# Attention and two expert layers on one core: first expert's weights behind the last pair's copies, routing of batch 0 from unit 64 on, two expert blocks with half of their second layer in plain fp32

## The chip, the core and the metric

The program runs on one core of a Trainium2 chip. Its engines work side by side, each through its own list of instructions: TensorE for matrix products (PE; PEld is its weight load), VectorE (DVE), ScalarE (ACT), GpSimd (POOL) and SyncE (SP), which here issues most of the DMA transfers. The metric is the time of one execution on the device in microseconds (us), the median over runs.

## What is computed

Attention feeds a layer of routed experts, which feeds a layer in which every token uses every expert. All of it is fp32.

```python
# q, k, v: 2 batches, 8 heads, 576 rows, 64 columns
q_rot, k_rot = rotate(q), rotate(k)
scores = scale * q_rot @ k_rot.T
attn = softmax(scores)
x = (attn @ v)            # -> 1152 tokens x 512

# experts 1: D=512, F=1024, E=8, one expert a token
logits = normed(x) @ normed(expert_emb).T / tau
expert_idx = argmax(logits, axis=1)
for e in range(E):
    mask = expert_idx == e
    h = maximum(x[mask] @ w1[e], 0)
    out[mask] = gate_w[mask] * (h @ w2[e])

# experts 2: all experts, weights P by 8 rounds of row and column scaling
for e in range(E):
    out += P[:, e:e+1] * (maximum(x @ w1[e], 0) @ w2[e])
```

## The kernel before

**Attention** works on eight pairs of heads. A head has five tiles of rows (four of 120, one of 96), so that a pair makes ten units, and units k = 0 to 79 run in one loop. A unit computes scores (L245), their maxima on DVE (L251), the exponentials on ACT (L257), transposes them (L279) and multiplies with the values (L302). The operands of pair i, kd and qd, are laid out ahead, during pair i - 1: POOL splits the numbers (L217) and SP copies them, kd in the unit with k % 10 = 3 (L226) and qd in that with k % 10 = 5 (L224). Pair 7 starts with unit 70.

**Routing** of batch 0 runs beside the loop. `route_half(0)` is a generator of small DVE instructions, some products and a few DMAs; once a unit, `next(trickle)` (L719) runs it to its next yield, behind the exponentials of the unit before and ahead of this unit's scores. It finds each token's expert (L470 to L474), ranks the tokens of each expert with products of triangles of ones (rp, L479 to L481), picks the expert with most tokens (`choose`, L419), reads its number into a register of SP and issues eight loads of that expert's weights, four of w1 and four of w2, 512 KB each (`fetch`, L83, into raw1 and raw2). `pre_tokens` then gathers 128 of its tokens on POOL (L458), and `pre_x` (L647) transposes them into xp. `take_out` takes these tokens out of the counts.

**The pre-block** computes those 128 tokens ahead of the routing of batch 1, in plain fp32, directly from the weights as they are loaded: `pre_l1` in eight pieces (L660), `pre_turn` (ReLU and transposes, L668 to L673), `pre_l2` in eight pieces (L680).

**The blocks.** After batch 1 is routed, `blocks` (L546 to L554) works out which expert each of nine blocks of 128 tokens belongs to, and `run_blocks` (L993) works through them. Here fp32 products are made of three cheaper ones: a matrix is split into a rounded part and the rest (weights: whi by an ACT copy at L843, wlo by a DVE subtraction at L836, two pieces for w1 and two for w2 in a block; tokens xh, xl at L861 and L862; hidden h into hh and hl at L888 and L889), and the products are hi with hi, lo with hi and hi with lo (L871 for layer 1, L901 for layer 2). In step i of the loop PE does the first layer of block i, the transposes of block i + 1's tokens (L858) and the second layer of block i - 1, while DVE, ACT and SP prepare the weights of the block after. `expert(i, ...)` loads the weights of block i only if its expert is another than that of block i - 1; whether it is, a register decides, and SP passes through the instruction in either case. A ninth block of four groups of at most 32 tokens, with loads of its own (qw, L923), is worked into the gaps. The pieces raw_77 and raw_78 hold w1, raw_79 and raw_80 w2.

**Order.** On PE, DVE, ACT and POOL instructions run in the order of the code, on SP too up to the head of the blocks. A load on SP waits until its target is free, and all that stands behind it on SP waits as well. Each DMA of SP also waits for the one eight before it.

**The end.** From about 353 us on the second expert layer runs (L1414, L1468), with PE busy without a gap.

## Time and profile before

| | us |
|---|---|
| median of 3 runs (1127.18 to 1128.1) | 1127.88 |
| profiled execution, its own time | 1128.22 |
| its span, first to last instruction | 1126.4 |
| PE busy, of the span | 1092.8 (97%) |
| DVE busy | 777.3 (69%) |
| ACT busy | 454.2 (40%) |
| POOL busy | 146.9 (13%) |
| mean granted clock of PE | 0.990 |

The shares are means over stages that differ. A stretch in which PE is not busy is where time may be lost, and the timeline tells what ended it: in brackets behind an instruction stands the idle time of its engine ahead of it and what released it. A releaser is inferred, and a wait for several things is put down to the one that came last by the profile. The granted clock is 1.00 at 2.4 GHz and 0.50 at 1.2 GHz.

### The profile page before, as it was taken

How to read it: one execution, taken by the hardware profiler on the slowest of the kernel's cores; microseconds unless marked ns; L12 is line 12 of the kernel's file. 1: busy time of each engine (PE TensorE's matmuls, PEld its weight loads, DVE VectorE, ACT ScalarE, POOL GpSimd, SP SyncE). 2: the span in 40 equal slices, each digit the busy share in tenths (PEclk: the TensorE clock that was granted, in tenths of full speed). 3: DMA queues.
4: the chain of work that ended last, by engine and by line, in shares of the span. 5: the costliest groups of instructions: out<-in, count | busy, mean ns of one | idle time of the engine just before them, and what ended most of it. 6: DMA issues, size and time to landing. Idle time of an engine off the chain costs nothing.

```text
span 1126.4 us, 16853 instructions
## 1 busy us (share of the span) xinstructions
PE 1092.8 (97%) x6588; PEld 926.4 (82%) x6589; DVE 777.3 (69%) x1277; ACT 454.2 (40%) x739; POOL 146.9 (13%) x115
## 2 busy tenths in 40 slices
PE   8999869999998999999999999999999999999998
PEld 4777655676766998999889998899988999899986
DVE  5767855988644488766776667766777667776665
ACT  4666625668653452233222332233322333223320
POOL 7664400253201000400000000000000000000000
PEclk9999989999998999999999999999999999999999
DMA  8676541165786011111111111111111111111102
GB/s 243 175 185 190 150 157 43 61 258 216 287 291 177 23 56 38 38 56 39 56 38 38 58 46 48 38 39 56 51 45 38 42 53 57 38 38 49 28 1 84
DMA packets 74980, 102.05 MB, mean 91 GB/s; under 512 B 5128, under 2 KB 46600, under 8 KB 74128
## 3 DMA queue, kind: packets, MB, share of 16 engines
q1 hardware_dynamic: 72528, 94.09, 27.4%
q0 software_dynamic: 1760, 5.77, 1.5%
q8 instruction: 54, 0.88, 0.3%
q10 hardware_dynamic: 608, 1.07, 0.3%
q14 instruction: 30, 0.25, 0.1%
HBM read 106.08 MB, written 7.60 MB: 101 GB/s over the span
## 4 chain that ended last, share of the span: by engine, by line
PE 67%; DMA 1%; DVE 0%; SPq 0%; ACT 0%; issue 0%
PE o L1468 35%; PE d L1414 30%; PE d L1431 2%; DMA g<-yd 1%; PE o L1358 0%; PE d L1311 0%; DVE acc L1479 0%; PE o L1389 0%; SPq L1297 0%; DVE st L1445 0%; DVE h L1456 0%; ACT h L1455 0%; PE o L1311 0%; PE o L1377 0%; PE o L1364 0%
## 5 line engine op out<-in xcount | busy, mean ns | idle before, releaser
L1468 PE MATMUL o<-w,h 128*128 128x512 f32 x1728 | 399.6, 390 | 0.3 <-DVE acc L1479 0.3
L1468 PEld LDWEIGHTS o<-w,h 128*128 128x128 f32 x1728 | 322.1, 188 | 66.2 <-DVE acc L1479 0.7
L1414 PE MATMUL d<-yq,w 128*128 128x288 f32 x2520 | 340.0, 294 | 0.0
L1414 PEld LDWEIGHTS d<-yq,w 128*128 128x128 f32 x2520 | 336.8, 188 | 2.6 <-ACT st L1442 0.2
L1479 DVE SCALAR_TENSOR_TENSOR acc<-o,P,acc 128x512 f32<-128x512 f32 x252 | 189.1, 751 | 77.1 <-PE o L1468 76.5
L1180 ACT ACTIVATE w<-raw 128x512 fp32r<-128x512 f32 x124 | 70.8, 574 | 129.9 <-DVE raw L1225 129.9
L1456 DVE SCALAR_TENSOR_TENSOR h<-st,h 128x576 fp32r<-128x576 f32 x90 | 68.0, 755 | 52.7 <-ACT h L1455 52.6
L1455 ACT ACTIVATE h<-st 128x576 fp32r<-128x576 f32 x90 | 61.5, 683 | 98.0 <-DVE st L1445 98.0
L836 DVE TENSOR_TENSOR wlo<-raw,whi 128x2048 fp32r<-128x2048 f32 x36 | 81.9, 2289 | 24.3 <-ACT whi L843 23.1
L1442 ACT ACTIVATE st<-d 128x576 f32<-128x576 f32 x90 | 58.7, 652 | 91.0 <-PE d L1414 89.0
L251 DVE TENSOR_REDUCE nb<-s 120x1 f32<-120x576 f32 (+1 forms) x80 | 60.3, 754 | 46.7 <-PE s L245 34.1
L1455 ACT ACTIVATE h<-d 128x576 fp32r<-128x576 f32 x38 | 24.7, 650 | 160.1 <-PE d L1414 158.0
L1445 DVE TENSOR_TENSOR st<-st,d 128x576 f32<-128x576 f32 x90 | 67.4, 749 | 23.9 <-PE d L1414 23.7
L257 ACT ACTIVATE p<-s,nb 120x576 f32<-120x576 f32 (+1 forms) x80 | 59.1, 739 | 60.3 <-DVE nb L251 57.7
L1181 DVE TENSOR_TENSOR w<-raw,w 128x512 fp32r<-128x512 f32 x124 | 76.9, 622 | 0.4 <-ACT w L1180 0.4
L245 PE MATMUL s<-kd,qd 128*120 128x288 f32 x280 | 55.5, 322 | 12.9 <-DMA wgk<-wg 9.6
L843 ACT ACTIVATE whi<-raw 128x2048 fp32r<-128x2048 f32 x32 | 61.3, 1917 | 14.4 <-PE h L871 9.9
L1456 DVE SCALAR_TENSOR_TENSOR h<-d,h 128x576 fp32r<-128x576 f32 x38 | 28.8, 757 | 53.7 <-ACT h L1455 53.7
L245 PEld LDWEIGHTS s<-kd,qd 128*120 128x120 f32 x280 | 39.4, 182 | 25.5 <-issue 14.5
L302 PE MATMUL o<-ph,vr 120*64 120x288 f32 x320 | 46.9, 418 | 0.0
L1241 DVE TENSOR_TENSOR w<-raw,w 128x1024 fp32r<-128x1024 f32 x32 | 39.2, 1225 | 5.6 <-ACT w L1240 5.6
L285 DVE COPY ph<-pt 120x480 f32<-120x480 f32 x64 | 41.4, 647 | 1.9 <-PE pt L279 1.9
(322 smaller groups left out, 1074.0 us busy)
## 6 DMA issues: line engine op xcount, KB each, us to landing
raw<-w1a SPq DMA_DIRECT2D x36, 512.0 KB
raw<-w2a SPq DMA_DIRECT2D x36, 512.0 KB
raw<-w1b SPq DMA_DIRECT2D x64, 256.0 KB
raw<-w2b SPq DMA_DIRECT2D x32, 512.0 KB
qw<-w1a SPq DMA_DIRECT2D x16, 512.0 KB
qw<-w2a SPq DMA_DIRECT2D x16, 512.0 KB
kd<-hl SPq DMA_DIRECT2D x28, 288.0 KB
r<-qk SPq DMA_DIRECT2D x6, 1152.0 KB
```

The source lines that it names most:

```text
L245: T.matmul(s[:m, h, :HS], qd[:, j, t * QT:t * QT + m], kd[:, j, x, h * HS:(h + 1) * HS], start=(x == 0), stop=(x == 1))
L251: V.tensor_reduce(nb[:m], s[:m, :, :HS], axis=AX.XY, op=ALU.max, negate=True)
L836: V.tensor_tensor(lo, raw, hi, op=ALU.subtract)
L843: A.activation(hi, raw, AF.Copy)
L1180: A.activation(hi, src, Copy)
L1181: V.tensor_tensor(lo, src, hi, op=ALU.subtract)
L1414: T.matmul(d[1][:, q, :QW], wv[:, wx, which, k], yq[yx][:, YQ[p], k, q * QW:(q + 1) * QW], start=new and k == 0 and (wx, yx) == (0, 0), st ...
L1445: V.tensor_tensor(halves(st[x]), halves(st[x]), mid(d), op=ALU.add)
L1455: A.activation(hi, src, AF.Relu)
L1456: V.scalar_tensor_tensor(lo, src, 0.0, hi, op0=ALU.max, op1=ALU.subtract)
L1468: T.matmul(d, hs[n][:, r, hx, t * 128:(t + 1) * 128], w2[n][:, wx, r], start=(r == 0 and (hx, wx) == (0, 0)), stop=(r == 1 and hx == 1))
L1479: V.scalar_tensor_tensor(a, d, p, a, op0=ALU.mult, op1=ALU.add)
```

## The change

1. Routing of batch 0 starts after unit 64 and not 56, and its yields are put together, 15 steps rather than 21. The instructions are the same. SP's eight loads of the expert's weights so come behind the copies qd of the last pair.
2. `pre_x` stands behind the loop and the drained routing, not in unit 77.
3. The routing of batch 1 has fewer yields, and three of them are taken ahead of the last rows, not five.
4. `pre_l1(2, 8)` stands in one piece ahead of batch 1's remaining routing; the splitting of the first w1 on DVE stands ahead of `blocks()`; only the first half of the first w2 is split; `pre_l2` is cut at 5 and 7, not at 3 and 5.
5. Blocks 0 and 1 (i < RAW = 2) take the second half of their second layer, k = 4 to 7, in plain fp32: raw2p[1] as loaded, with hf, an fp32 copy of the turned h by ACT in place of the second half of hh. There is no splitting of raw2p[1] and no second half of hl for these blocks.
6. Since these blocks read raw2p[1] itself, the load of w2 for blocks 1 and 2 is issued behind the second layer of block 0 and 1.

```diff
-        yield V.reduce_max(out=top, in_=tot, axis=AX.X)
-        V.tensor_tensor(own, tot, top.to_broadcast([QT, E]), op=ALU.is_equal)
+        V.reduce_max(out=top, in_=tot, axis=AX.X)
+        yield V.tensor_tensor(own, tot, top.to_broadcast([QT, E]), op=ALU.is_equal)
...
-            if k == 56:
+            if k == 64:
                 trickle = route_half(0)
-            if k == 77:
-                pre_x()
...
         for _ in trickle:
             pass
+        pre_x()
...
-        for _ in range(5):
+        for _ in range(3):
             next(routes)
...
-    def block_turn(h):
+    def block_turn(h, raw=False):
...
+            if raw and n == 1:
+                hf = mp.tile([128, F], F32, tag="qx", bufs=1, name="hf")
+                A.activation(hf[:, c], pt, AF.Copy)
+                return hh, hl_, hf
...
-        todo = [(k, a, b) for k in range(KF) for a, b in ((0, 0), (0, 1), (1, 0))]
+        todo = [(k, a, b) for k in range(2 * len(w)) for a, b in ((0, 0), (0, 1), (1, 0))]
...
+        for k in range(2 * len(w), KF):
+            T.matmul(p, h[2][:, k * 128:(k + 1) * 128], raw2[k // 2][:, (k % 2) * 512:(k % 2 + 1) * 512],
+                     start=False, stop=(k == KF - 1))
...
-            pre_l2(0, 3)
+            pre_l2(0, 5)
             x = block_x(xb[0])
-            pre_l2(3, 5)
+            pre_l2(5, 7)
...
-                    pre_l2(5, KF)
+                    pre_l2(7, KF)
...
-                    h = block_turn(hn)
-                    split_low(raw2p[1], *w2[1])
+                    h = block_turn(hn, True)
                     w2 = pieces(w2)
-                    expert(1, raw2, w2a, 256)
...
+                if 0 < i <= RAW:
+                    expert(i, raw2, w2a, 256)
                 if here:
-                    s2 = split(raw2p)
+                    s2 = split(raw2p[:1 if i < RAW else 2])
                     next(s2)
...
-                    next(s2)
-                    w2 = next(s2)
-                    expert(i + 1, raw2, w2a, 256)
-                    h = turned[0] if i == hi - 1 else block_turn(hn)
+                    *_, w2 = s2
+                    if i >= RAW:
+                        expert(i + 1, raw2, w2a, 256)
+                    h = turned[0] if i == hi - 1 else block_turn(hn, i < RAW)
...
-        first_w1, first_w2 = [pair(), pair()], [pair(), pair()]
+        first_w1, first_w2 = [pair(), pair()], [pair()]
...
-        pre_l1(2, 7)
+        pre_l1(2, 8)
         for _ in routes:
             pass
         xb = [block_in(i) for i in range(3)]
-        pre_l1(7, 8)
-        blocks()
         for raw, (hi, lo) in zip(raw1p, first_w1):
             split_low(raw, hi, lo)
+        blocks()
```

On SP, in the attention's seventh pair, before: the copies kd of the last pair, the reading of the expert's number (bei) into a register, then the first of the eight loads (those of raw_77 to raw_80), with qd only behind the last of them.

```order
L226 DMA kd<-hl 64x2x576 x4
L426 TENSOR_LOAD bei
L426 ISA x2
L83 ISA
L83 DMA raw_77<-w1a 128x1024
```

The same place now:

```order
L227 DMA kd<-hl 64x2x576 x4
L225 DMA qd<-hl 64x576 x4
L427 TENSOR_LOAD bei
L427 ISA x2
L84 ISA
L84 DMA raw_77<-w1a 128x1024
```

The four copies qd have moved ahead of the register and of the eight loads.

On ACT, from the second layer of block 0 to the second of block 1, before (y is a block's result, whi a half of the weights rounded, hh the turned h):

```order
L907 ACTIVATE y<-yp,gate 128x512
L843 ACTIVATE whi<-raw_79 128x2048
L907 ACTIVATE y<-y,gate 128x512
L843 ACTIVATE whi<-raw_80 128x2048
L888 ACTIVATE hh<-ht 128x512 x2
L843 ACTIVATE whi<-raw_77 128x2048
```

The same place now:

```order
L915 ACTIVATE y<-yp,gate 128x512
L844 ACTIVATE whi<-raw_79 128x2048
L915 ACTIVATE y<-y,gate 128x512
L893 ACTIVATE hh<-ht 128x512
L891 ACTIVATE hf<-ht 128x512
L844 ACTIVATE whi<-raw_77 128x2048
```

The copy of raw_80 is gone, and hf stands for the second half of hh.

On PE, the end of block 0's second layer, before:

```order
L901 MATMUL y<-whi,hh 128x512
L901 MATMUL y<-wlo,hh 128x512
L901 MATMUL y<-whi,hl__2312 128x512
L539 LDWEIGHTS slot
L539 MATMUL gp<-gv,slot 128x16
```

The same place now:

```order
L906 MATMUL y<-whi,hh 128x512
L906 MATMUL y<-wlo,hh 128x512
L906 MATMUL y<-whi,hl__2309 128x512
L909 MATMUL y<-raw_80,hf 128x512 x4
L541 LDWEIGHTS slot
L541 MATMUL gp<-gv,slot 128x16
```

Of the 24 split products the last 12 are gone, and four plain ones on raw_80 stand at the end.

## Rows read from the trace of the kernel before

**Rows 1.** Page, the chain that ended last: shares of the span by line.

```profile
PE o L1468 35%; PE d L1414 30%; PE d L1431 2%; DMA g<-yd 1%; PE o L1358 0%; PE d L1311 0%; DVE acc L1479 0%; PE o L1389 0%; SPq L1297 0%; DVE st L1445 0%; DVE h L1456 0%; ACT h L1455 0%; PE o L1311 0%; PE o L1377 0%; PE o L1364 0%
```

**Rows 2.** Timeline of PE: start, duration, engine, line, operation, operands, count, [idle, releaser].

```profile
102.75 0.78 PE L245 MATMUL s<-kd,qd 128*120 128x288 f32 x4
...
106.69 0.80 PE L245 MATMUL s<-kd,qd 128*120 128x288 f32 x4
...
121.77 0.78 PE L245 MATMUL s<-kd,qd 128*120 128x288 f32 x4
...
124.19 0.79 PE L245 MATMUL s<-kd,qd 128*120 128x288 f32 x4 [1.23 <-ACT p L257]
...
133.73 0.72 PE L313 MATMUL pr<-turn_enb,u 128*120 128x144 f32 x4 [1.33 <-DVE x L366]
...
153.39 1.28 PE L245 MATMUL s<-kd,qd 128*120 128x288 f32 x4 [9.62 <-DMA wgk<-wg]
...
159.52 0.79 PE L245 MATMUL s<-kd,qd 128*120 128x288 f32 x4
```

**Rows 3.** Timeline of SP: issues of the last two pairs' copies.

```profile
115.29 3.80 SPq L224 DMA_DIRECT2D qd<-hl  x4
...
137.21 2.14 SPq L83 DMA_DIRECT2D raw<-w1a  x4
...
142.99 3.40 SPq L224 DMA_DIRECT2D qd<-hl  x4
```

**Rows 4.** Windows: length, busy by engine (instructions), granted clock, DMA share, GB/s.

```profile
203.00:236.00 33.00, 29.85 (x183) 23.09 (x182) 31.21 (x69) 19.68 (x19) 7.51 (x6) 1.00 0.24 89
...
150.00:152.00 2.00, 0.00 (x0) 0.00 (x0) 0.00 (x0) 0.00 (x0) 0.00 (x0) 0.50 1.07 256
...
238.00:240.00 2.00, 2.00 (x6) 1.59 (x5) 2.00 (x2) 0.88 (x2) 2.00 (x1) 0.50 1.00 397
```

**Rows 5.** Timeline of PE, ACT and DVE around block 1's second layer.

```profile
219.61 0.48 PE L901 MATMUL y<-whi,hh 128*128 128x512 f32 x1
...
225.18 0.91 PE L539 MATMUL gp<-gv,slot 120*128 120x16 bf16 x30
...
236.13 0.66 PE L858 MATMUL xt<-io,xb 128*128 128x128 f32 x4 [2.28 <-DVE hl__2563 L889]
...
250.81 0.47 PE L901 MATMUL y<-whi,hh 128*128 128x512 f32 x1
...
241.16 1.92 ACT L843 ACTIVATE whi<-raw 128x2048 fp32r<-128x2048 f32 x1 [2.28 <-PE y L901]
...
248.62 1.28 DVE L889 TENSOR_TENSOR hl__2706<-ht,hh 128x512 fp32r<-128x512 f32 x2
```

**Rows 6.** Timeline: routing instructions on DVE, both batches; POOL beside them.

```profile
120.70 1.91 DVE L472 TENSOR_TENSOR eq<-eq,cs 120x40 f32<-120x40 f32 x1
...
130.54 1.37 DVE L423 TENSOR_TENSOR own<-own,cs 120x8 f32<-120x8 f32 x1
...
188.09 0.20 DVE L472 TENSOR_TENSOR eq<-eq,cs 120x40 f32<-120x40 f32 x1
...
119.92 2.64 POOL L208 TENSOR_TENSOR r<-r,tb 128x1152 f32<-128x1152 f32 x1
```

**Rows 7.** Timeline: the pre-block's first layer on PE; splitting on DVE.

```profile
189.37 4.54 PE L660 MATMUL hp<-raw,xp 128*128 128x512 f32 x10
...
195.21 1.10 PE L660 MATMUL hp<-raw,xp 128*128 128x512 f32 x2
...
197.51 4.50 DVE L836 TENSOR_TENSOR wlo<-raw,whi 128x2048 fp32r<-128x2048 f32 x2
```

**Rows 8.** Timeline: loads of w2, blocks 3 and 4; ACT's copy.

```profile
245.43 0.08 SPq L83 DMA_DIRECT2D raw<-w2a  x1
...
260.93 0.39 SPq L83 DMA_DIRECT2D raw<-w2a  x1
...
271.98 1.91 ACT L843 ACTIVATE whi<-raw 128x2048 fp32r<-128x2048 f32 x1 [0.43 <-DMA raw<-w1a]
```

More of the change, by code (lines that the diff above doesn't have):

```diff
@@ L31 @@
 NS = 9
+RAW = 2
 NG = 4
@@ L428, in choose @@
             fetch(raws, src, m, reg[0])
-        yield V.tensor_tensor(own, col("rev"), top.to_broadcast([QT, E]), op=ALU.is_equal)
-        V.tensor_tensor(w5, ohb[:, 0, :NQ], over(own, 1, [QT, NQ, E]), op=ALU.mult)
-        yield V.reduce_sum(out=ox, in_=w5, axis=AX.X)
+        V.tensor_tensor(own, col("rev"), top.to_broadcast([QT, E]), op=ALU.is_equal)
+        yield V.tensor_tensor(w5, ohb[:, 0, :NQ], over(own, 1, [QT, NQ, E]), op=ALU.mult)
+        V.reduce_sum(out=ox, in_=w5, axis=AX.X)
         V.scalar_tensor_tensor(rk[:, 0], ox, -float(BLK), rk[:, 0], op0=ALU.mult, op1=ALU.add)
-        yield V.tensor_single_scalar(pre, rk[:, 0], -0.5, op=ALU.is_lt)
+        V.tensor_single_scalar(pre, rk[:, 0], -0.5, op=ALU.is_lt)
     def take_out():
-        yield V.tensor_single_scalar(keep_, rk[:, 0], -0.5, op=ALU.is_gt)
+        V.tensor_single_scalar(keep_, rk[:, 0], -0.5, op=ALU.is_gt)
         sh = [QT, NQ, E]
         yield V.tensor_tensor(ohb[:, 0, :NQ], ohb[:, 0, :NQ], over(keep_, 2, sh), op=ALU.mult)
-        yield V.tensor_tensor(tri, col("tri", a=E), over(own, 1, [QT, E, E]), op=ALU.max)
+        V.tensor_tensor(tri, col("tri", a=E), over(own, 1, [QT, E, E]), op=ALU.max)
         V.tensor_scalar(tot, own, -1.0, 1.0, op0=ALU.mult, op1=ALU.add)
@@ L468, in route_half @@
         sh = [QT, NQ, E]
-        yield V.reduce_max(out=mx[:, b], in_=lg[:, b], axis=AX.X)
+        V.reduce_max(out=mx[:, b], in_=lg[:, b], axis=AX.X)
         yield V.tensor_tensor(eq, lg[:, b], over(mx[:, b], 2, sh), op=ALU.is_equal)
-        yield V.tensor_tensor(eq, eq, col("revm", a=NQ), op=ALU.mult)
+        V.tensor_tensor(eq, eq, col("revm", a=NQ), op=ALU.mult)
         yield V.reduce_max(out=fi, in_=eq, axis=AX.X)
@@ L486, in route_half @@
             V.tensor_copy(tot, rp[:, NQ])
-        yield V.tensor_tensor(w5, rp[:, :NQ], ohb[:, b, :NQ], op=ALU.mult)
+        V.tensor_tensor(w5, rp[:, :NQ], ohb[:, b, :NQ], op=ALU.mult)
+        yield
         if b > 0:
@@ L901, in block_l2 @@
             T.matmul(p, h[a][:, k * 128:(k + 1) * 128], w[k // 2][b][:, (k % 2) * 512:(k % 2 + 1) * 512],
-                     start=(n == 0), stop=(n == len(todo) - 1))
+                     start=(n == 0), stop=(n == 3 * KF - 1))
+        for k in range(2 * len(w), KF):
+            T.matmul(p, h[2][:, k * 128:(k + 1) * 128], raw2[k // 2][:, (k % 2) * 512:(k % 2 + 1) * 512],
+                     start=False, stop=(k == KF - 1))
         return p
```

## The prediction

> **What bounds the kernel now.** I read three views in this order: the chain that ended last, the windows by stage, and then the timeline at each place where TensorE (PE) sat idle. The chain [rows 1] is almost wholly the products of the last stage (L1468 35%, L1414 30%): from about 353 us on PE never rests, so this end can't be shortened by the change, and whatever is saved ahead of it moves the end by as much. Ahead of it two places matter. The first is the last pair of heads in the attention. The scores of unit 70 start at 153.39 after 9.62 us of idleness [rows 2]. The row names the small load of wg; the real releaser is the queue ahead of it. On SP the copies of kd are issued, then four loads of w1a from 137.21 and four of w2a (8 x 512 KB), and only then the four copies qd that unit 70 reads, at 142.99 [rows 3]. In the pair before, nothing stands in between: qd goes out at 115.29 [rows 3] and unit 60 starts at 121.77 without a wait [rows 2]. The second place is the start of the expert blocks, 203 to 236, where DVE is busy 31.21 of 33 us [rows 4] and PE waits 2.28 us for it at 236.13 [rows 5].
>
> **The change, part by part.**
>
> *Weights behind the copies.* The idle 9.62 us go. So does what follows them: the granted clock is 0.50 (the 1.2 GHz level) in 150 to 152 and later [rows 4], after PE had done nothing since 143.8. Units 70 to 72 take 159.52 - 153.39 = 6.13 us, units 50 to 52 take 106.69 - 102.75 = 3.94 [rows 2]. That is 2.2 us. Together 11.8. The weights themselves are hidden: issued at about 147 of the new time, 4.2 MB at the rate they have now (eight issues from 137.21, all in flight by 143, unit 70 released at 153.4: at most 16 us [rows 2, 3]) land by 163 at the latest, while the products that read them stand at 189.37 [rows 7], in the new time near 177, but for a first pair some 4 us ahead, which reads only the first of the loads. Even the upper bound leaves 9 us.
>
> *Routing of batch 0 from unit 64 on, in 15 steps.* Where it ran before, units 60 to 70, PE lost two short waits, 1.23 us at 124.19 and 1.33 at 133.73 [rows 2]: 2.56 us. Each lies behind routing instructions on DVE that took 1.91 us (L472, 120.70) and 1.37 (L423, 130.54), while L472 takes 0.20 in batch 1 [rows 6]. At those times POOL was at work (L208, 2.64 us from 119.92) [rows 6]; in the new place POOL has no such work but one splitting of qd. So the slow forms should mostly go. But the same DVE work is now squeezed into fewer units, two or three instructions a step ahead of the maximum that the next scores need. Cost: nothing, if DVE's slack takes it, up to the 2.56 us again. I put 1.6, nearer the upper end because the steps are denser. The four transposes of the gathered tokens stand behind the loop now, with an ACT copy of which PE may wait: 0 to 0.7 us, 0.4 taken. The gather itself is issued five units before that and shares the DMA engines with the weights; it has about 8 us.
> Sum of the stage: -9.6 - 2.2 - 2.6 + 1.6 + 0.4 = **-12.4 us**, bounds -10.8 (all costs at their top) and -14.4 (none).
>
> A rule of the Trainium skill bears on the squeeze: "SBUF — State Buffer", section "Who interferes with whom", says that a DVE instruction with two SBUF inputs contends with a GpSimd instruction that reads SBUF, and that the later one is blocked. The 1.91 against 0.20 us agree with it. By that rule alone the 1.6 would be near zero, and the stage -14; no row shows the steps in their new place, so the sum keeps 1.6.
>
> *The head of the expert part.* The pre-block's first layer runs in one piece, so its ReLU, turn and second layer start some 1.5 us earlier: its last two products now begin at 195.21, after two places' matmuls, 1.3 us behind the first ten [rows 7]. That gain isn't PE's alone: from 195 on DVE has the splitting of w1, 4.50 us from 197.51 [rows 7], and behind it its 31.21 of 33 us [rows 4]. The splitting starts about 2 us earlier against the rest, because the blocks' numbers now come behind it, and the numbers' own 2 us then come later. I take 0, bounds -1.5 and +0.5.
>
> *Blocks 0 and 1.* On PE each loses 12 products of (225.18 - 219.61)/24 = 0.232 us [rows 5] and gains 4 plain products of two instructions; ten such instructions take 4.54 us, the last with its drain, so 0.43 to 0.45 each [rows 7], 8 x 0.43 = 3.4. Per block 3.4 - 2.8 = +0.7, twice +1.4. DVE loses per block one splitting of 2.29 us (half of the 4.50 [rows 7]) and one of 0.64, so 5.9 us in all; ACT two copies of 1.92. The DVE relief takes the 2.28 us at 236.13, and with them the half clock of 238 to 240 [rows 4]: 8 products at 0.43 rather than 0.23, 1.6 to 1.9 us. Block 1's second layer then ends at +0.7 + 0.7 - 2.3 - 1.8 = -2.7 us, say -2.4, against before.
>
> *What is late next.* Block 1 reads the second half of w2 as it was loaded, up to the end of that layer. So the load for block 2 may be issued only then, and on SP it stands behind the loads for block 4. In this data the load is not taken (the blocks share an expert): such an issue takes 0.08 us at 245.43 against 0.39 for one that moves data at 260.93 [rows 8]. Still, ACT's copy of w2 for block 2, at 241.16 before [rows 5], must wait for it: at about 242.1 + L, L being the time from the issue of a load that is not taken to its semaphore. Behind that copy follow in order: DVE's splitting, ACT's copy and splitting of the other half, and the halves of the turned h, 248.62 before and about 248.3 + L now. Block 2's second layer then starts at about 250.2 + L against 250.81 [rows 5], with PE idle 1.2 + L ahead of it. No row shows L. Its lower bound is 0. The upper is what a load has to wait behind block 4's real ones, some 3 us. I take 0.3, since an issue of 0.08 us leaves no room for the descriptors of a real one. So of the 2.4 us that the relief wins, most is given back: **-0.3**, from -2.4 to +4.3 (L = 3 and a half clock again, 1.9).
>
> *The rest of batch 1's routing, and blocks 2 to 8*, have the same instructions; from 250 us on PE is the bound there, and nothing is added to it.
>
> Total: -12.4 + 0 - 0.3 = -12.7 us. The profiled execution took 1128.22 us with a span of 1126.4; the median of the runs is 1127.88, 0.3 less. So the changed kernel's span should be near 1113.8 and its median near **1115.2 us**.
>
> **The rivals.**
> 1. *The blocks pay in full.* If block 2's copy and splitting aren't late (L near 0 and DVE ahead by its 5.9 us), PE doesn't idle before block 2 and the 2.4 us stay, and the pre-block's 1.5 may show too: 1127.9 - 12.4 - 2.4 - 0.5 = 1112.6. For it speaks that DVE is what PE waits for in this stretch [rows 5] and that DVE loses 5.9 us of work; against it that block 2's chain begins on ACT, behind a load, and not on DVE.
> 2. *Block 2's load is late.* L = 2 to 3: PE idles 3 to 4 us, as long as the 2.28 that cost the clock before, and pays 1.9 more: 1127.9 - 12.4 - 0.6 + 2.5 + 1.9 = 1119.3. The page "DMA: Bandwidth & Descriptors", section "Anatomy of one DMA — SWDGE (gpsimd) path" of the Trainium skill, puts a fixed 2.0 us on a DMA, most of it completion; an estimate with it would be L = 2 and 1118.8. Whether a load that is not taken pays that, no row shows.
> 3. *The stall goes only in part.* Copies and steps collide in units 65 to 70: DVE's maxima come late by the squeezed steps in each of five units by the 1.2 to 1.3 us that the two waits showed [rows 2], 6 us of the 12.4 come back: 1121.3. Against it: the copies of pair 6 beside the first steps of routing made no wait at unit 60.
> 4. *Slower.* The loads for blocks 1 and 2 are real transfers. Then each is issued only behind a second layer and lands about 11 us later, as block 4's w2 does (issued 260.93, its copy on ACT at 271.98 [rows 8]). Its user comes about 3.5 us behind the issue, so PE stands 7.5 us twice: -12.7 + 15 = +2.3, 1130.2. It decides once a load takes over 10 us. The 0.08 us issues speak against it.
> 5. *It doesn't do what it says*, the weights still ahead of the copies: 1127 to 1129. The order on SP excludes it.
>
> **How the numbers follow.** Forecast 1115.2 (1113.5 to 1117.2): 0.50. Rival 1: 0.18. Rival 2: 0.17. Rival 3: 0.11. Rivals 4 and 5: 0.02 each. The range takes in rivals 1 and 2: **1111.8 to 1119.5**. A measurement of this kernel can tell about 0.2%, 2.3 us: faster than 1125.6 is 0.97 (all but rivals 4 and 5 and the far end of 3), same 0.02, slower 0.01.
>
> **What would show it.** In the profile after: the weights of the pre-block on SP behind qd; no wait for a DMA at the scores of unit 70; a granted clock of 1.00 (2.4 GHz) from 143 to 160; the first product of the pre-block 12 us earlier. In units 65 to 79 the waits of PE for DVE should sum to under 2 us. The transposes of tokens ahead of block 1's second layer without the 2.28 us, and a new wait of 1 to 2 us of the transposes ahead of block 2's, with the copy of w2 on ACT released by a DMA. Wrong it would be if unit 70 still waited over 2 us, if that last wait were over 3 us, or if PE waited for the weights at the pre-block.

## The result and the profile after

The changed kernel took 1114.85 us (median of 4 runs, 1114.64 to 1115.58), the kernel before 1127.53 (4 runs, 1126.46 to 1128.1) beside it: 12.7 us less, a ratio of 0.989 with a 95% interval of 0.9873 to 0.9907. The forecast was 1115.2, in a range of 1111.8 to 1119.5. The profiled execution took 1114.84 us with a span of 1113.1, 13.3 below the 1126.4 of before. A second set of 4 runs of the changed kernel (e11_changed below) had a median of 1115.24.

The page of the changed kernel, PE's line of the engines and the shares of the chain that ended last, to be read against [rows 1]:

```profile
PE 1090.0 (98%) x6581; PEld 921.8 (83%) x6581; DVE 768.7 (69%) x1273; ACT 449.8 (40%) x737; POOL 140.7 (13%) x115
...
PE o L1475 35%; PE d L1421 30%; PE d L1438 2%; DMA g<-yd 0%; PE d L1318 0%; PE o L1365 0%; PE d L1315 0%; DVE acc L1486 0%; PE o L1396 0%; PE o L1318 0%; DVE st L1452 0%; DVE h L1463 0%; ACT h L1462 0%; PE o L1384 0%; PE o L1371 0%
```

The end is the same: the two products of the last stage still carry the chain, and PE is busy 98% of a shorter span. So what was saved was saved ahead of it.

The timeline of PE at units 50, 60, 65, 70, 72 and 79 and at the pre-block's first product, as in [rows 2] (the line numbers are one higher in the changed kernel):

```profile
103.54 0.79 PE L246 MATMUL s<-kd,qd 128*120 128x288 f32 x4
...
122.58 0.79 PE L246 MATMUL s<-kd,qd 128*120 128x288 f32 x4
...
132.17 0.79 PE L246 MATMUL s<-kd,qd 128*120 128x288 f32 x4
...
142.00 0.79 PE L246 MATMUL s<-kd,qd 128*120 128x288 f32 x4
...
146.35 0.80 PE L246 MATMUL s<-kd,qd 128*120 128x288 f32 x4
...
162.31 0.77 PE L246 MATMUL s<-kd,qd 128*96 128x288 f32 x4
...
173.13 1.13 PE L662 MATMUL hp<-raw,xp 128*128 128x512 f32 x2
```

Unit 70 starts at 142.00 with no bracket behind it: it waits for nothing. The timeline of SP shows why, against [rows 3]; the qd copies of the last pair go out at 135.10, and the eight loads come 5 us behind them:

```profile
135.10 3.84 SPq L225 DMA_DIRECT2D qd<-hl  x4
144.13 1.98 SPq L84 DMA_DIRECT2D raw<-w1a  x4
146.30 2.85 SPq L84 DMA_DIRECT2D raw<-w2a  x4
```

The windows of the stretch that held the stall, and of the start of the blocks, against [rows 4]:

```profile
143.00:153.00 10.00, 9.05 (x71) 6.86 (x70) 8.81 (x27) 5.71 (x13) 0.00 (x0) 1.00 0.76 277
...
203.00:236.00 33.00, 33.00 (x186) 24.62 (x186) 23.82 (x47) 18.37 (x17) 8.62 (x7) 0.96 0.63 221
191.00:224.00 33.00, 31.06 (x179) 23.08 (x178) 26.59 (x66) 17.76 (x19) 4.81 (x5) 0.95 0.39 131
```

The granted clock is 1.00 where it was 0.50. The second window has the same times as before, but shows the program some 12 us further on; the third, 12 us earlier, shows about the stretch of the program that [rows 4] show. In it DVE is busy 26.59 us where it was 31.21. But the mean clock there is 0.95. To see where the time came from, the lengths between the same instructions of both traces, starts taken from [rows 2, 5, 7] and from the fences of this section (the head's and the blocks' further down):

| stretch | before | after | difference | forecast |
|---|---|---|---|---|
| unit 50 to unit 65 | 31.4 | 28.6 | -2.8 | -2.6 |
| unit 65 to unit 70 | 19.2 | 9.8 | -9.4 | -9.6 |
| unit 70 to unit 72 | 6.1 | 4.4 | -1.8 | -2.2 |
| unit 72 to the pre-block's first product | 25.4 | 26.8 | +1.4 | +2.0 |
| to block 0's first layer | 18.4 | 18.5 | +0.2 | 0 |
| to the end of block 0's second layer | 21.9 | 24.2 | +2.2 | +0.7 |
| to the transposes of block 3's tokens | 11.0 | 7.9 | -3.0 | -2.3 |
| to the transposes of block 4's tokens | 14.3 | 15.2 | +0.9 | +1.3 |
| from there to the end | 875.9 | 874.2 | -1.8 | 0 |

Starts that no fence shows: unit 65 before 134.19, unit 79 174.99, the pre-block's first product 184.91, block 0's first layer 203.27, block 4's tokens 250.46; after, block 0's second layer ends at 215.81 (225.18 before [rows 5]). The forecast's 2.0 us of costs in the new place stand whole in the fourth line, though the routing's steps run in the two lines above it too. The attention's four lines sum to -12.6 us, the head and the blocks to +0.3. The last line and 0.8 us ahead of unit 50 lie outside what the change touches; such stretches differ between executions of kernels that have the same work there (last section).

### The profile page after: what moved, and what is told of

It reads as the page before. It is cut to its first block, busy times and chain, and to the rows that moved or that the text cites. A ratio compares the mean times of both kernels' runs of the same rounds, so it can differ in the third digit from the quotient of the medians.

```text
span 1113.1 us, 16829 instructions
## 1 busy us (share of the span) xinstructions
PE 1090.0 (98%) x6581; PEld 921.8 (83%) x6581; DVE 768.7 (69%) x1273; ACT 449.8 (40%) x737; POOL 140.7 (13%) x115
## 4 chain that ended last, share of the span: by engine, by line
PE 68%; DMA 0%; DVE 0%; ACT 0%; issue 0%; SPq 0%
PE o L1475 35%; PE d L1421 30%; PE d L1438 2%; DMA g<-yd 0%; PE d L1318 0%; PE o L1365 0%; PE d L1315 0%; DVE acc L1486 0%; PE o L1396 0%; PE o L1318 0%; DVE st L1452 0%; DVE h L1463 0%; ACT h L1462 0%; PE o L1384 0%; PE o L1371 0%
## 5 line engine op out<-in xcount | busy, mean ns | idle before, releaser
L1475 PEld LDWEIGHTS o<-w,h 128*128 128x128 f32 x1728 | 322.1, 188 | 66.2 <-DVE acc L1486 0.7
L837 DVE TENSOR_TENSOR wlo<-raw,whi 128x2048 fp32r<-128x2048 f32 x34 | 77.5, 2289 | 28.4 <-ACT whi L844 28.3
```

Of the source, the lines that this page charges most:

```text
L837: V.tensor_tensor(lo, raw, hi, op=ALU.subtract)
L1475: T.matmul(d, hs[n][:, r, hx, t * 128:(t + 1) * 128], w2[n][:, wx, r], start=(r == 0 and (hx, wx) == (0, 0)), stop=(r == 1 and hx == 1))
```

## The experiments

Each is compared with the kernel before, run beside it. "To unit 70" and "to block 5" are read from the profiled execution: from the start of unit 50's scores to those of unit 70 and to the transposes of block 5's tokens. This takes out the spread of the program's start and end.

| kernel | median us | before beside it | to unit 70 | to block 5 |
|---|---|---|---|---|
| before | 1127.53 | | 50.6 | 162.0 |
| changed | 1114.85 | 1127.53 | 38.5 | 149.7 |
| e11_changed (the same program) | 1115.24 | 1128.14 | 38.4 | 148.2 |
| e1_route | 1115.27 | 1127.52 | 38.5 | 149.3 |
| e3_noraw | 1117.21 | 1127.52 | 38.4 | 150.5 |
| e4_cuts | 1113.34 | 1127.52 | 38.5 | 147.4 |
| e12_cuts (the same program) | 1113.22 | 1128.14 | 38.4 | 148.0 |
| v_raw_only | 1114.65 | 1127.52 | 38.4 | 147.8 |
| e5_fetch | 1116.69 | 1128.18 | 40.9 | 152.5 |
| e6_warm | 1128.24 | 1128.18 | 51.2 | 163.0 |
| e7_first | 1114.48 | 1128.18 | 38.4 | 147.8 |
| e8_best | 1114.34 | 1128.18 | 38.4 | 147.9 |
| e9_real | 1128.22 | 1128.14 | 38.4 | 161.0 |
| e10_cuts_first | 1112.98 | 1128.14 | 38.4 | 146.7 |

**Which part carries the change: e1_route.** The routing part alone on the kernel before.

```diff
...
-            if k == 56:
+            if k == 64:
                 trickle = route_half(0)
-            if k == 77:
-                pre_x()
...
+        pre_x()
...
```

> The kernel before with the routing part alone: routing of batch 0 from unit 64 on in 15 steps, weights behind the copies qd, pre_x behind the loop, three steps of batch 1 ahead of the last rows. Head and blocks as before. Theory (the attention carries the whole change, the term of -12.4 us): 12.0 to 12.8 us faster than before, no DMA wait at unit 70, the 2.28 us wait ahead of block 1's second layer still there. Rival (the blocks carry some of it): 8 to 11 us faster, with new waits in units 65 to 79.

It took 12.25 us off (ratio 0.9888, 0.9871 to 0.9904), as the theory had it. To unit 70 it is as the changed kernel to 0.1 us, and the wait of the blocks is untouched, as the timeline of PE shows for the transposes of block 3's tokens:

```profile
222.99 0.66 PE L858 MATMUL xt<-io,xb 128*128 128x128 f32 x4 [2.28 <-DVE hl__2563 L889]
```

The 2.28 us of [rows 5] stand there as before. So the routing part by itself explains the whole difference of the medians; what head and blocks add, the medians don't show.

**What the routing part is made of: e5_fetch and e6_warm.** In the first, routing still starts after unit 56, and the loads are moved behind the copies (what follows them in the routing comes two units later as well):

```diff
         V.tensor_scalar(bei[:, NB + 1 + NG:], top[0:1], -1.0, float(E), op0=ALU.mult, op1=ALU.add)
+        yield
+        yield
         reg.append(nc.sync.value_load(bei[0:1, NB + 1 + NG:NB + 2 + NG], min_val=0, max_val=E - 1))
```

> The kernel before with one thing moved: two empty steps ahead of the reading of the expert's number, so that the eight loads come in unit 66, behind the copies qd of the last pair. Routing still starts after unit 56. Theory (of the -12.6 us of the routing part, 9.4 are the idle stall and 1.8 the clock behind it, and 2.8 the waits for slow routing instructions that stay here, less some 1.4 of costs): unit 70 starts without a wait for a DMA, units 60 to 65 still take about 2.8 us more than in the changed kernel, and the time falls by 9.5 to 11 us. Rival (the slow routing instructions aren't the cause of the waits in 60 to 65, the weights' loads or their copies are): 12 to 13 us.

The median fell by 11.5 us (0.9894, 0.9877 to 0.991), a little above the expected range. In the profiled execution it is 11.7 from unit 50 to the pre-block's first product (173.22), and 9.5 to block 5, since the clock fell to half in the pre-block (below). The timeline of PE, units 60, 61, a product of unit 64 and units 65 and 70:

```profile
121.75 0.79 PE L245 MATMUL s<-kd,qd 128*120 128x288 f32 x4
...
124.20 0.79 PE L245 MATMUL s<-kd,qd 128*120 128x288 f32 x4 [1.25 <-ACT p L257]
...
133.66 0.72 PE L313 MATMUL pr<-turn_enb,u 128*120 128x144 f32 x4 [1.25 <-DVE x L366]
134.12 0.79 PE L245 MATMUL s<-kd,qd 128*120 128x288 f32 x4
...
143.63 0.78 PE L245 MATMUL s<-kd,qd 128*120 128x288 f32 x4
```

Unit 70 no longer waits, so the order of SP's queue alone made the stall. The waits of [rows 2] at 124.19 and 133.73 are still there, 1.25 us each, and units 60 to 65 take 12.4 us as before, against 9.6 in the changed kernel. So these 2.8 us come from moving the routing, not the loads. Most of them are spent again in the new place: from unit 65 to the pre-block's first product e5_fetch takes 39.1 us and e1_route 40.9, which is 1.8 more. From unit 50 to the pre-block it is 82.2 us before, 70.5 in e5_fetch and 69.5 in e1_route: the order of the queue is worth 11.7 us there, the move of the routing 1.0.

What the routing's slow instructions wait for is shown by DVE and POOL in the changed kernel, against [rows 6]:

```profile
134.70 0.50 DVE L473 TENSOR_TENSOR eq<-eq,cs 120x40 f32<-120x40 f32 x1
...
142.56 0.15 DVE L424 TENSOR_TENSOR own<-own,cs 120x8 f32<-120x8 f32 x1
...
133.73 1.41 POOL L218 TENSOR_TENSOR hl<-r,hl 128x576 fp32r<-128x576 f32 x1 [2.53 <-ACT hl L217]
```

The same instruction that took 1.91 us takes 0.50, the one that took 1.37 takes 0.15. In all three slow cases DVE ends with POOL's instruction: 120.70 + 1.91 = 122.61 and 119.92 + 2.64 = 122.56 [rows 6]; 130.54 + 1.37 = 131.91 and, in the kernel before, a splitting on POOL (L217) at 130.47 + 1.41 = 131.88; here 134.70 + 0.50 = 135.20 and 133.73 + 1.41 = 135.14. That agrees with what the Trainium skill says under "SBUF — State Buffer", section "Who interferes with whom": one of the two has the shared port to itself, and the other waits until it is done. No run took POOL's work away, so this rests on three coinciding ends.

In the second, small products without a use fill the stall of the kernel before:

```diff
+                    if k == 70:
+                        keep_warm(wz, 42)
                     s = scores(n, t)
```

> The kernel before with 42 extra small products without a use ahead of the scores of unit 70, about 9 us, which fill the stall for the copies. Nothing is computed from them. Theory (1.8 to 2.2 us of the change are the half clock that follows the idle stall): unit 70 starts when it did, the granted clock stays 1.00 behind it, units 70 to 72 take 3.9 to 4.4 us rather than 6.1, and the time falls by 1.5 to 2.5 us. Rival (the units after the stall are slow for their own work or for the loads): no change within 0.7 us.

The timeline of PE, a window behind the filling and one in the pre-block:

```profile
143.93 9.24 PE L321 MATMUL warm<-wz 128*128 128x512 bf16 x42
154.20 0.76 PE L245 MATMUL s<-kd,qd 128*120 128x288 f32 x4 [1.04 <-DMA wgk<-wg]
...
158.54 0.80 PE L245 MATMUL s<-kd,qd 128*120 128x288 f32 x4
```

```profile
154.00:156.00 2.00, 1.80 (x17) 1.69 (x17) 0.93 (x2) 0.14 (x1) 0.00 (x0) 1.00 0.02 4
...
196.00:198.00 2.00, 1.97 (x8) 1.57 (x8) 1.93 (x4) 1.06 (x2) 1.70 (x2) 0.51 0.37 113
```

Unit 70 starts 0.6 us later in its own time (51.2 against 50.6), then the clock is 1.00 where it was 0.50, and units 70 to 72 take 4.3 us rather than 6.1. So the half clock is the idle time's doing and costs 1.8 us here; in e5_fetch the same two units take 3.9 us (143.63 to 147.57), which would make it 2.2. In the total nothing shows (ratio 0.9995, 0.9984 to 1.0005), which is the rival's number. In the profiled execution the clock fell to 0.51 in the pre-block instead, and the stretch from its first product to block 5 is 2.2 us longer than before. Whether that is so in the other executions no trace shows. The run shows what the clock does behind the stall, and nothing on the whole.

**The head: e3_noraw, e4_cuts, v_raw_only.** Block 0 took 2.2 us more and not 0.7. The timeline of PE in the changed kernel, from the pre-block's second layer to block 4's tokens:

```profile
185.51 4.56 PE L682 MATMUL yp<-raw,hpt 128*128 128x512 f32 x10 [0.69 <-ACT hpt L675]
...
191.66 1.03 PE L872 MATMUL h<-whi,xh 128*128 128x512 f32 x2
...
199.80 0.66 PE L887 MATMUL ht<-io,h 128*128 128x128 f32 x4 [0.80 <-ACT h L878]
201.60 0.66 PE L887 MATMUL ht<-io,h 128*128 128x128 f32 x4 [1.14 <-DVE xl L863]
...
223.72 0.64 PE L859 MATMUL xt<-io,xb 128*128 128x128 f32 x4
...
238.06 0.66 PE L941 MATMUL qxt<-io,xb 128*128 128x128 f32 x4 [1.15 <-DMA xb<-xd,idx]
238.95 0.66 PE L859 MATMUL xt<-io,xb 128*128 128x128 f32 x4 [0.23 <-DVE hl__2682 L894]
```

The pre-block's second layer starts 13.3 us earlier than at 198.83, 1.5 more than its first product: the forecast gain of the one-piece first layer. Then it is lost: PE waits 0.80 us for block 0's ReLU and 1.14 us for DVE's half of block 1's tokens, at 199.80 and 201.60. Before, six instructions of pre_l2 stood there, and PE waited 0.49 us (213.26); now two do. The change was undone there:

```diff
-            pre_l2(0, 5)
+            pre_l2(0, 3)
             x = block_x(xb[0])
-            pre_l2(5, 7)
+            pre_l2(3, 5)
...
-                    pre_l2(7, KF)
+                    pre_l2(5, KF)
```

> The changed kernel with pre_l2 cut at 3 and 5 as before (0 to 3, tokens, 3 to 5, and 5 to 8 in block 0) and all else as changed. Theory (in the changed kernel the last piece of pre_l2, one product, no longer fills the time in which PE waits for block 0's ReLU and block 1's tokens, so that 1.9 us of idleness and some 1.6 us of half clock stand in 199 to 206): these go, 2 to 3.5 us faster than the changed kernel, near 1112. Rival (the gap is made by DVE, which has the splitting first and the numbers behind it): within 0.7 us of the changed kernel.

The median was 1113.34 (ratio to before 0.9872, 0.9855 to 0.9888), 1.5 us less than the changed kernel's 1114.85: between the theory's 2 to 3.5 and the rival's 0.7. The pair was repeated side by side:

> The changed kernel with pre_l2 cut as before, once more, beside the changed kernel on one chip. Theory (the cuts take 0.6 to 1.5 us of idleness in block 0 and with it the chance of half a clock): 1 to 2.5 us faster than the changed kernel in this call. Rival (the difference of the first call was one of executions): within 0.7 us.

1113.22 against 1115.24 of the changed kernel beside it, 2.0 us less, with ranges that don't touch (1112.65 to 1113.94 and 1114.15 to 1115.84): the theory. The timeline of PE, at block 0's tokens and in block 0:

```profile
188.77 0.66 PE L859 MATMUL xt<-io,xb 128*128 128x128 f32 x4 [0.95 <-DMA xb<-xd,idx]
...
196.89 2.74 PE L682 MATMUL yp<-raw,hpt 128*128 128x512 f32 x6
199.47 0.60 PE L887 MATMUL ht<-io,h 128*128 128x128 f32 x4
200.51 0.66 PE L887 MATMUL ht<-io,h 128*128 128x128 f32 x4 [0.44 <-DVE xl L863]
```

In block 0, 0.44 us of the 1.94 are left, but a wait of 0.95 us for the gather of block 0's tokens has come, which the longer first piece of pre_l2 had covered. So the idle time is only 0.55 us less. From the pre-block's second layer to the end of block 0's second layer PE takes 28.15 us in e12_cuts and 28.70 in e11_changed, both at full clock, and 30.3 in the first profile of the changed kernel, which has the half clock. The rest of the 2.0 us between the medians these traces don't show; half clocks in the executions without a profile may be part of it.

The other two undo more at once. e3_noraw has routing and new head without the plain fp32 halves:

```diff
-RAW = 2
...
-                    s2 = split(raw2p[:1 if i < RAW else 2])
+                    s2 = split(raw2p)
```

> The changed kernel with the plain fp32 halves undone: blocks 0 and 1 split all of their w2 again, its loads issued where they were; routing and the new order of the head (pre_l1 in one piece, splitting ahead of the blocks' numbers, pre_l2 cut at 5 and 7) kept. Theory (the new head neither gains nor loses more than 0.5 us by itself): as the routing part alone, 12.0 to 13.0 us faster than before. Rival (the new head opens a gap in block 0, 0.80 and 1.14 us idle in the changed kernel and half the clock behind it): 9 to 11 us faster.

It is 10.3 us faster than before, 1.9 less than the routing part alone: the rival. Its trace has the same gap in block 0, 0.80 and 1.18 us, and the half clock behind it; from block 0's first layer to the end of its second it takes 23.5 us and e1_route 21.9. But the profiled execution was the longest of five (1114.93 to 1118.29), and e1_route's (1113.73 to 1117.03) overlap them, so that the 1.9 us is not a firm size. v_raw_only has routing and halves with the head as before:

```diff
-        pre_l1(2, 8)
+        pre_l1(2, 7)
         for _ in routes:
             pass
         xb = [block_in(i) for i in range(3)]
+        pre_l1(7, 8)
+        blocks()
         for raw, (hi, lo) in zip(raw1p, first_w1):
             split_low(raw, hi, lo)
-        blocks()
```

> Routing part and plain fp32 halves, with the whole head as before (pre_l1 to 7 and the last piece behind, blocks' numbers ahead of the splitting, pre_l2 cut at 3 and 5; only the first half of the first w2 split). Theory (the halves win the 2.4 us of the wait ahead of block 1's second layer once the gap in block 0 isn't there): 14 to 15.5 us faster than before, 1112.5 to 1114. Rival (DVE gives it back elsewhere in the head): 12 to 13 us faster, as the changed kernel.

To block 5 it is 14.2 us shorter than before, 1.5 better than the routing part alone: so much the halves win in these two profiles, and 0.7 to 1.0 of it is the half clock behind the 2.28 us of e1_route (next experiment). The median, 12.9 less, is the rival's number; its runs spread over 3.4 us (1113.51 to 1116.95). What the halves win is read from the traces only.

**The clock in the gap: e11_changed.** The same program again.

> The changed kernel itself once more, beside the others of this call on one chip. Theory (the half clock behind the gap in block 0 comes in some executions and not in others, since another kernel with the same 1.94 us of idleness kept its clock): the median within 1 us of 1114.85; in the profile the clock in block 0 either at half for some 4 us again or at full, and then block 0 1.7 us shorter. Rival (it belongs to this order of instructions): half again.

Windows from 202 to 206, first of the changed kernel's profile, then of this one's:

```profile
202.00:204.00 2.00, 2.00 (x9) 1.57 (x8) 2.00 (x2) 1.90 (x3) 0.00 (x0) 0.59 0.01 4
204.00:206.00 2.00, 2.00 (x7) 1.57 (x6) 1.86 (x10) 0.69 (x1) 0.00 (x0) 0.55 0.00 0
```

```profile
202.00:204.00 2.00, 2.00 (x11) 1.61 (x10) 2.00 (x2) 1.93 (x2) 0.00 (x0) 1.00 0.02 4
204.00:206.00 2.00, 2.00 (x11) 1.65 (x10) 1.83 (x11) 0.48 (x1) 0.00 (x0) 1.00 0.00 0
```

The idle time ahead is the same, 0.80 and 1.14 us. In the one execution the clock fell to half, in the other it stayed, and the trace to block 5 is 1.5 us shorter. Of the five profiles that have this gap, the half clock followed in two (the changed kernel, e3_noraw) and not in three (e11_changed, e7_first, e9_real). The 2.28 us of [rows 5] do the same: half clock behind them in the kernel before and in e1_route, full clock in e5_fetch, where it had fallen over the short waits of the pre-block instead. Two windows of e5_fetch, the first in the pre-block, the second behind the 2.28 us:

```profile
188.00:190.00 2.00, 2.00 (x3) 0.91 (x4) 2.00 (x2) 2.00 (x2) 1.70 (x2) 0.50 0.15 20
...
228.00:230.00 2.00, 2.00 (x10) 1.63 (x10) 1.93 (x6) 2.00 (x2) 1.10 (x1) 1.00 0.93 307
```

So a gap of about 2 us here carries a price that is paid in some executions. Behind the 1.94 us it is 1.6 us: from block 0's first layer to the end of its second the changed kernel takes 24.15 us in its first profile and 22.55 in its second. Behind the 2.28 us it is 0.7 to 1.0: from block 3's tokens to block 4's 14.3 us before, 13.4 in e5_fetch and 13.6 in e6_warm, where PE then waits 0.33 and 0.59 us for a gather instead. What decides it was not settled.

**What is late next: e7_first, e8_best, e10_cuts_first.** The quad is the ninth block, of four groups. In the changed kernel ACT's copy of block 2's w2 waits for its load, and SP tells why; ACT first, then SP:

```profile
231.68 1.92 ACT L844 ACTIVATE whi<-raw 128x2048 fp32r<-128x2048 f32 x1 [4.62 <-DMA raw<-w2a]
...
227.10 3.25 SPq L84 DMA_DIRECT2D raw<-w1a  x4
231.07 7.83 SPq L84 DMA_DIRECT2D raw<-w2a  x8
```

The load goes out at 231.07, behind block 4's load of w1, whose third part waits for DVE until 229.3; ACT starts 0.6 us behind the first issue and about 0.1 behind the end of the second (231.50 + 0.08), which is the one that completes its operand. So a load that is not taken costs next to nothing from issue to use, and its place on SP is what makes it late. e7_first issues the half whose target is free ahead of block 4's load:

```diff
+                    if 0 < i <= RAW:
+                        expert(i, raw2, w2a, 256, (0, 1))
                     expert(i + 2, raw1, w1a, 128)
...
-                    expert(i, raw2, w2a, 256)
+                    expert(i, raw2, w2a, 256, (2, 3))
```

> The changed kernel with the loads of w2 for blocks 1 and 2 in two parts: those of the first half, whose target is free, ahead of block 3's and 4's load of w1 on SP, those of the second half where all four stood. Theory (block 2's chain is late since its load stands on SP behind block 4's load of w1, which waits for DVE; ACT's wait of 4.62 us for it): that wait goes, the halves of the turned h come 3 to 4 us earlier, but the transposes of the quad's tokens still wait 1.15 us for their gather: 0.2 to 1 us faster than the changed kernel. Rival (a load that is not taken takes its time from issue to semaphore, wherever it stands): the wait only shrinks to 2 to 3 us and the time is the same.

ACT's wait of 4.62 us is gone, the copy standing in the row without a bracket:

```profile
224.08 1.94 ACT L844 ACTIVATE whi<-raw 128x2048 fp32r<-128x2048 f32 x1
...
235.22 0.66 PE L941 MATMUL qxt<-io,xb 128*128 128x128 f32 x4 [1.14 <-DMA xb<-xd,idx]
```

and PE waits the same 1.14 us for the gather of the quad's tokens. The median is 1114.48, 0.4 less than the changed kernel's, within the spread. So the theory's mechanism holds and the rival's doesn't; the times don't tell them apart. e8_best adds the old cuts and moves the quad's transposes behind block 2's second layer:

```diff
-                elif i == 3:
-                    quad_tokens()
...
                 elif i in (3, 4, 5, 6, 7):
+                    if i == 3:
+                        quad_tokens()
```

> The changed kernel with pre_l2 cut as before (0 to 3, 3 to 5, 5 to 8), the loads of w2 for blocks 1 and 2 in two parts as in the run before, and the transposes of the quad's tokens behind block 2's second layer rather than ahead of it. Theory (three waits in the expert blocks go: the gap in block 0, ACT's wait for block 2's w2 and PE's for the quad's gather): 3 to 4.5 us faster than the changed kernel, near 1111. Rival (the waits only move to the next block's transposes): 2 to 2.5 us, as with the cuts alone.

Neither number came: 1114.34 us is 0.5 less than the changed kernel's 1114.85. The rival's mechanism held, the waits moved. PE now waits 1.26 us at the transposes of block 4's own tokens, for their gather, and 0.69 at the quad's product:

```profile
235.83 0.63 PE L859 MATMUL xt<-io,xb 128*128 128x128 f32 x4 [1.26 <-DMA xb<-xd,idx]
...
243.04 1.92 PE L954 MATMUL q<-qw,qx 128*32 128x512 f32 x16 [0.69 <-ACT qx L943]
```

With the quad's transposes where they were, e10_cuts_first:

> The changed kernel with pre_l2 cut as before and the loads of w2 for blocks 1 and 2 in two parts; the transposes of the quad's tokens stay ahead of block 2's second layer. Theory (the two waits are independent, and PE then waits for the gather of the quad's tokens): at most 0.5 us faster than with the cuts alone. Rival (they add up): 1 to 2 us faster than with the cuts alone.

1112.98 us (1111.81 to 1114.24; ratio 0.9863, 0.9843 to 0.9882), 2.3 less than the changed kernel beside it and 0.2 less than the cuts alone: by the medians the theory. By the traces to block 5 it is 0.7 to 1.3 us shorter than the two profiles of the cuts alone (146.7, 147.4 and 148.0), which is nearer the rival. It is the fastest median of all, though not to be told from e12_cuts.

**The price of a real load: e9_real.** The loads of w2 for blocks 1 and 2 without their condition:

```diff
-                fetch(raws, src, n, reg[i], reg[i] != reg[i - 1])
+                fetch(raws, src, n, reg[i], None if raws is raw2 and i <= RAW else reg[i] != reg[i - 1])
```

> The changed kernel with the loads of w2 for blocks 1 and 2 made without their condition, so that the same 2.1 MB are really moved again behind block 0's and block 1's second layer. Theory (the prediction's rival for a slower kernel: a real load behind a second layer lands about 11 us after its issue, and its user comes 3.5 us behind it): two stalls of about 7.5 us, 12 to 18 us slower than the changed kernel, and ACT waits for the loads by the profile. Rival (they land beside the other work since DVE and the quad's loads leave room): under 6 us slower.

1128.22 us, 13.0 more than the changed kernel beside it and as slow as before (0.9998, 0.9983 to 1.0012). The timeline of ACT for both loads, of PE, and of SP for block 4's w1 and block 2's w2:

```profile
218.56 1.92 ACT L844 ACTIVATE whi<-raw 128x2048 fp32r<-128x2048 f32 x1 [1.94 <-DMA raw<-w2a]
...
240.66 1.91 ACT L844 ACTIVATE whi<-raw 128x2048 fp32r<-128x2048 f32 x1 [13.63 <-DMA raw<-w2a]
...
248.19 1.12 PE L859 MATMUL xt<-io,xb 128*128 128x128 f32 x4 [11.76 <-DVE hl__2682 L894]
...
226.51 3.41 SPq L84 DMA_DIRECT2D raw<-w1a  x4
230.11 2.57 SPq L84 DMA_DIRECT2D raw<-w2a  x4
```

The total is the theory's, the way to it is not: it is one stall of 11.76 us and not two of 7.5. Block 1's load is hidden but for 1.94 us on ACT, while block 2's goes behind block 4's real load of w1 and its first half lands some 10 us behind the issue at 230.11. The half clock behind the stall adds 1.7 us: from block 4's tokens to block 5's it is 16.0 us, and 14.3 in the changed kernel.

## Why the prediction was right, and where it wasn't

The main term was right in sum and in each part. The stall and the half clock are best read from e5_fetch, where the routing stays in units 60 to 65: there unit 65 to unit 70 is 9.7 us shorter (9.5 for 19.2) and unit 70 to unit 72 2.2 shorter (3.9 for 6.1), forecast 9.6 and 2.2. In the changed kernel these two lines are -9.4 and -1.8, since the routing's steps now stand in them. PE's waits for DVE in units 65 to 79 are 0.48 us (144.68) and 0.41 us (152.59), well under the 2 us that the prediction allowed. The two waits in units 60 to 65 gave -2.8 for -2.6. e1_route shows that the parts make the whole; e5_fetch and e6_warm show the order of the queue and the half clock apart. The weights are hidden, as said: no product of the pre-block waits for a load.

The costs in the new place were about right too, though the table's fourth line alone (+1.4 for +2.0) doesn't show it. Against e5_fetch, e1_route is 0.3 us longer from unit 65 to 70, 0.4 to unit 72, 0.1 to unit 79 and 0.9 to the pre-block: 1.8 for 2.0. The transposes of the gathered tokens have moved from the third of these stretches to the fourth; they cost 0.4 us more there (0.41 in e5_fetch, 0.82 with the 0.24 us of wait for ACT in e1_route), as forecast, which leaves 1.4 for the squeezed steps, put at 1.6. So moving the routing gained 1.0 us net, forecast 0.6. The bound of -10.8 of this stage doesn't follow from its terms: both costs at their top make -11.1.

The head was the part whose working had a gap, though its net came out right. It weighed the pre-block's earlier start against DVE's queue and put 0 for both. It left out what pre_l2's last three pieces, six instructions or 2.7 us, covered in block 0: PE's wait for the ReLU and for block 1's tokens. With one piece left there, the idle time grew from 0.49 to 1.94 us and took the earlier start back. In the first profile a half clock followed, and block 0 took +2.2 us for +0.7. In e11_changed, at full clock, the lines of head and blocks are +0.2, +0.6, -3.0 and +1.1, for 0, +0.7, -2.3 and +1.3. That the net came out near 0 was in part luck: of the two waits that took the start back, one is for DVE, as weighed, and one for the ReLU on ACT.

The blocks' two ends were right and partly for another reason. The 2.28 us and the half clock behind them went; that half clock had cost 0.7 to 1.0 us and not 1.8, since without it PE waits for a gather instead. Of the return, "PE idle 1.2 + L" ahead of block 2's second layer, 1.15 + 0.23 us came, but most of it for the gather of the quad's tokens, which the prediction doesn't name; the chain by ACT and DVE, which it does, came 0.23 us later still. L was put at 0.3 and is about 0.1. The sum there doesn't close: an idle time of 1.2 + 0.3 behind -2.4 makes -0.9 and not -0.3. From block 0's first layer to block 4's tokens e11_changed shows -1.3, and the first profile, with its half clock in block 0, +0.1.

The rivals: the blocks' full gain, 1112.6, is near what the kernels with the old cuts reach, 1113.0 to 1113.3, but by other terms, since block 2's return stays. The late load decided nothing, since L is small. The stall went whole. For the slower rival, e9_real shows the stated condition, real loads, and about the price, 13.0 us for 15, in one stall and not two: the queue behind another real load, not the distance to the second layer, makes the second load late.

## What to carry to other kernels

Look at which small transfer, needed next, stands in a queue behind large ones that are needed much later; here moving eight loads behind four copies was worth 11.7 of the 12.7 us up to the pre-block, and about 2 of them were the half clock after the idle time. When work is moved out of a stretch in which it is slow, count what it costs in the new one: 2.8 us were gained here and 1.8 paid. When pieces of independent work are moved to start something earlier, ask what they covered where they stood, and when they are moved back, what they covered in the new place. A gap of some 2 us may cost nearly twice its length in one execution and not in the next, so compare stretches of the trace from a common instruction before believing 1 or 2 us of a median.

## What the runs showed that was not expected

The granted clock behind the same idle time differs between executions of one program: 0.59 and 0.55 in two windows of the changed kernel's first profile, 1.00 in both of its second, behind 0.80 and 1.14 us of idleness in each. Behind 2.28 us it was 0.50 in the kernel before and 1.00 in e5_fetch.

Two stretches in which all these kernels have the same work differ between their profiles: unit 50 starts at 102.3 to 103.6 us, and from block 7's tokens to the second expert layer's first product (d<-yq) it is 64.3 to 68.0 us, 66.2 before and 64.3 in the changed kernel's first profile. From there to the end it is 763.4 us in every one. So the table's last line, -1.8, lies in the second of these stretches. PE waits there for the blocks' results to be read back (g<-yd): from the end of the last block's products to the first product on g it is 13.4 us before and 12.4 in the changed kernel's first profile. Why that differs was not looked into.
